# A fused adaLN, linear-attention and SwiGLU kernel: w_phi on ScalarE's queue, x's second chunk as one early load, silu and BD on GpSimd, and a new static order

## The chip, the cores and the metric

The kernel runs on one core of a Trainium2 chip. The metric is device time in microseconds of one launch. "Before" took 199.31 us (median of three runs, 198.96 to 199.45). The profile is one execution on the same chip, with a trace of every instruction of the engines: TensorE (PE, its weight loads PEld), VectorE (DVE), ScalarE (ACT), GpSimd (POOL) and SyncE (SP), which issues most of the DMAs.

## What is computed

One transformer layer on x of 2048 tokens by 512, in bf16. Six vectors of 512 come from a conditioning row c; they shift, scale and gate the two halves:

```python
mod = silu(c) @ w_mod                       # 6 x 512: sa, ca, ga, sb, cb, gb
h = layernorm(x) * (1 + ca) + sa
q, k, v = heads(h @ wqkv)                   # 32 heads of 16
pq, pk = q @ w_phi, k @ w_phi               # one 16x16 matrix per head
phi_q = concat(softmax(pq), softmax(-pq)); phi_k likewise
kv = phi_k.T @ v;  z = phi_k.sum(tokens)
o = (phi_q @ kv) / (phi_q @ z + 1e-6)
x = x + ga * (o @ wo)
h = layernorm(x) * (1 + cb) + sb
x = x + gb * ((silu(h @ w_gate) * (h @ w_up)) @ w_down)   # inner width 1376
```

## The kernel before

**Tiling.** The tokens are 16 tiles of 128, in four chunks of four tiles (x_c0 to x_c3, called x0 to x3 here). Weights stay in SBUF. All matmuls are bf16 into six one-bank PSUM tiles (one_ps) and a two-bank one (kv_ps).

**Start.** silu(c) is made as follows: four 1-row matmuls turn c into columns (L450), ScalarE takes exp(-c) into sig (L459), VectorE adds one, takes the reciprocal and multiplies (L454 to L456, f_silu). w_mod's first two parts then give modA, the shift and scale of the first half: eight 128x1 matmuls for each of four slices of 128 rows (L473), and a copy on VectorE (L478). Meanwhile w_phi is folded into wk: 16 small matmuls spread w_phi over the partitions (phx, L499), VectorE multiplies with a mask to the block-diagonal BD (L502), TensorE transposes wk (L519), ScalarE or VectorE copies it out (WT, L523), TensorE multiplies with BD (L530), and ScalarE or VectorE copies the folded wk back (L533, L534). wq is folded likewise a little later, with its transposes by DMA (L292).

**First norm.** For each tile VectorE takes bn_stats and their aggregate (L348, L349). The reciprocal root is taken by ScalarE (Ln, Exp, L377 and L378) or by GpSimd (power, L381 and L382), a reduction on VectorE gives the negative product with the mean (L384), and the normalize into xn runs on GpSimd, ScalarE or VectorE (L398, L396, L392). The tiles 0 to 5 are transposed by TensorE (L563, L414) and shifted and scaled on their way out of PSUM into hT (L566, L567, L422); the tiles from 6 on are transposed by DMA (L577) and shifted and scaled from SBUF (L585 to L590).

**K, V and Q.** Per tile: four matmuls for K (L619) and V (L623), two exponentials on ScalarE (L634), sums on VectorE (S, L640), a reciprocal (L644 to L646), va on VectorE (L650), a large multiply of e on GpSimd (L657), and then eight matmuls that add to kv_ps (L663). Q tiles are alike (L686, L690, L694, L696, L697, L701), and their result is transposed by DMA into pT (L705). After tile 15's kv accumulation VectorE masks the sum into KVZ (L790, L792).

**Second half.** Attention per tile (L824), its reciprocal A (L827) and product (L828) on VectorE, a transpose, the projection by wo (L857, wo having been multiplied by the gate on GpSimd, L780), the residual, the second norm, and then the SwiGLU part in units of one, two or four tiles (L909 gate and up, L916 silu, L919 or L923 and L925 for the product, L955 for the last 96 columns, L987 down, L997 and L1001 for gate and residual, and the stores at L1007).

**What sets the order.** Every step is announced by pl.op(alternatives, reads, writes, us, fn). A step may have several alternatives, each an engine with a planned duration. ORDER is a list written out by hand: number // 4 is the step, in the sequence of the calls, and number % 4 the alternative taken. Plan.run walks ORDER, gives each step the earliest start that its planned durations allow, chooses PSUM and SBUF slots, and emits all instructions by planned start. Each engine, and SyncE's queue ("XBAR" in the plan), works in the sequence in which ORDER names its steps. Where the plan finds TensorE idle in the first 90 us, fill() adds matmuls of ones into unused PSUM space (L1054). "later" (L289) is a load that SyncE issues at the place that ORDER gives it. One load is outside the plan: c_row, issued by ScalarE at L286, ahead of its table load (L319).

The loads in SyncE's sequence before: x0 (512 KB), wk (512 KB), w_phi (16 KB, 128 bytes per partition), w_mod in three loads (512, 256, 256 KB), x1 in two loads of 256 KB, x2, wq, wv, x3 (512 KB each). Then wq's transposes, and later the rest of w_mod, wo, w_gate, w_up and w_down, among the transposes.

Of the kernel before, what the change touches and what calls it, by code (L numbers as in the profile page):

```python
# [7 lines left out]
BF16 = mybir.dt.bfloat16  # L8
# [6 lines left out]
P = 128  # L15
# [20 lines left out]
def fm_size(m):  # L36
# [5 lines left out]
DMA_LN1 = 6  # L42
FILL_FROM, FILL_TO, FILL = 1.3, 90.0, 0.85
# [3 lines left out]
    0, 4, 48, 188, 72, 80, 8, 12, 16, 76, 20, 60, 52, 204, 228, 84, 56, 220, 172, 64, 208, 89, 92, 98, 156, 232, 176, 224, 24, 212, 104, 180, 193,  # L47
    28, 161, 236, 100, 184, 240, 196, 108, 217, 40, 246, 112, 164, 148, 116, 120, 124, 153, 36, 250, 32, 200, 268, 140, 168, 132, 128, 276, 316,
    252, 272, 68, 260, 144, 280, 136, 520, 264, 256, 324, 285, 320, 524, 328, 44, 424, 488, 428, 288, 560, 528, 464, 380, 492, 333, 600, 568, 294,
    298, 480, 432, 300, 472, 484, 336, 564, 468, 476, 368, 496, 342, 308, 532, 436, 346, 536, 304, 500, 541, 392, 440, 348, 608, 312, 384, 548, 445,  # L50
    604, 572, 510, 388, 828, 768, 404, 577, 452, 772, 544, 872, 372, 820, 376, 812, 776, 1344, 584, 506, 552, 513, 940, 518, 448, 460, 408, 412,
    804, 362, 358, 456, 396, 580, 780, 366, 944, 816, 864, 354, 904, 596, 824, 400, 868, 556, 808, 640, 832, 636, 612, 785, 792, 592, 836, 840, 908,
    788, 617, 644, 588, 1020, 876, 704, 800, 1340, 858, 1028, 648, 1024, 950, 796, 624, 881, 916, 620, 652, 416, 629, 962, 953, 888, 632, 860, 958,
    853, 1060, 921, 736, 656, 912, 1032, 846, 1188, 884, 712, 708, 900, 928, 716, 964, 1037, 744, 1228, 1268, 740, 1276, 924, 660, 1044, 850, 896,
    1308, 748, 1304, 933, 1040, 664, 1192, 1232, 893, 1200, 1360, 420, 1052, 936, 1318, 668, 720, 988, 1272, 1056, 993, 1240, 1196, 1049, 752, 1352,
    1205, 1325, 1212, 1328, 1208, 1224, 1280, 1313, 1236, 1322, 1245, 1252, 1336, 1356, 1220, 1285, 1364, 1248, 1264, 724, 1520, 1600, 1217, 1524,
    1369, 1292, 1604, 1528, 1260, 1348, 1004, 1560, 728, 1257, 1288, 1372, 1297, 1532, 1300, 1008, 1376, 1608, 1612, 1384, 1537, 1544, 1540, 1564,
    1816, 1388, 1617, 1620, 1640, 968, 1552, 1381, 1644, 1572, 1556, 1064, 1549, 1624, 1652, 1577, 1632, 1568, 1124, 1584, 1332, 1132, 1128, 1648,
    1580, 1592, 1596, 972, 1657, 1136, 976, 672, 1660, 1068, 996, 1636, 1589, 756, 1664, 1629, 1672, 732, 1072, 1669, 1676, 676, 1824, 980, 760,
    1828, 1092, 680, 1001, 1832, 1100, 984, 1680, 1836, 684, 1856, 1860, 1096, 1076, 1812, 1864, 1156, 1104, 1108, 1160, 1808, 1744, 2164, 1820,  # L60
    2168, 764, 1080, 1084, 2172, 1868, 1872, 1392, 1164, 1876, 1400, 2176, 688, 1748, 1424, 1112, 1116, 1880, 2180, 1688, 2184, 1488, 692, 1088,
    1884, 1396, 1712, 1888, 1120, 2416, 1684, 2188, 1140, 696, 1168, 1432, 1892, 2420, 700, 1752, 1776, 2424, 1716, 1898, 1172, 1456, 1492, 1144,
    1496, 1148, 1012, 1720, 1908, 1428, 1912, 1464, 2428, 1900, 1904, 2432, 2216, 1176, 2192, 2436, 2220, 2224, 2196, 2012, 2440, 1784, 2228, 1936,
    1152, 2016, 1460, 1180, 1780, 2200, 1016, 2204, 1952, 1500, 1916, 2020, 2232, 1940, 1944, 1956, 2237, 1948, 2444, 2208, 2024, 1404, 1960, 1184,
    2214, 2468, 2028, 1436, 2512, 2516, 1964, 1920, 1968, 2240, 1504, 2032, 2520, 2257, 1988, 2472, 2250, 1972, 2524, 1992, 1408, 1976, 2448, 1440,
    2246, 2253, 2296, 1980, 2528, 2316, 1924, 2452, 2036, 1984, 2260, 2040, 2532, 1444, 2304, 1412, 1448, 1416, 1452, 2352, 2536, 2044, 2300, 2456,
    1928, 2476, 2324, 2320, 1508, 1420, 1788, 2048, 2460, 2280, 2328, 1692, 2936, 1512, 1932, 2052, 2264, 2308, 2480, 2284, 2940, 2540, 2268, 2272,
    2288, 2944, 2056, 1516, 2332, 2544, 2484, 2924, 2360, 2564, 2292, 1848, 2928, 2340, 2932, 1792, 2948, 2064, 2568, 2548, 2312, 2060, 2336, 1724,
    2552, 2490, 2368, 2068, 2344, 2088, 2465, 1996, 2356, 2104, 2572, 2576, 2348, 2392, 1696, 2364, 2976, 2580, 2000, 2128, 2096, 1468, 1472, 2585,
    2072, 2556, 1728, 2980, 1476, 2492, 2984, 2372, 2276, 2506, 2112, 1732, 2124, 1481, 2952, 1756, 2988, 2561, 2588, 2510, 2132, 3032, 3036, 2605,  # L70
    1700, 1484, 3040, 2594, 2956, 1796, 2376, 2396, 2092, 2498, 1704, 2400, 2601, 2108, 2501, 2597, 2992, 1736, 2136, 2076, 3020, 2380, 2704, 2808,
    3024, 2080, 2720, 3028, 2960, 2404, 2116, 2997, 2964, 2668, 2648, 2816, 2100, 3044, 2724, 1708, 2652, 1760, 2728, 1740, 2732, 2968, 2676, 2974,
    2664, 2672, 3072, 2680, 3048, 3076, 3444, 1764, 2656, 2712, 2812, 2736, 3080, 3000, 2608, 2120, 3448, 2756, 1801, 3452, 2820, 3432, 3052, 3084,
    1804, 3056, 2760, 2744, 3060, 2140, 2660, 2764, 2824, 2628, 2612, 3436, 2616, 3064, 3088, 2408, 2144, 3013, 3006, 3440, 2700, 2620, 2084, 3094,
    3009, 2772, 2768, 2708, 2740, 1768, 3069, 3456, 2632, 3540, 3096, 2004, 2780, 1853, 2776, 3544, 2784, 2716, 3460, 2148, 3105, 2152, 3484, 3101,
    3017, 3548, 3488, 3492, 2792, 2684, 1772, 2636, 2688, 2748, 3464, 3114, 3528, 3532, 3110, 2752, 2788, 3536, 2692, 3468, 2640, 3552, 2796, 3116,
    3472, 2800, 3268, 3264, 3212, 3220, 2008, 3272, 2696, 3120, 2804, 3136, 3140, 3496, 3208, 3500, 3276, 3144, 3556, 3560, 3172, 3244, 3564, 3216,
    3476, 3568, 2624, 3482, 3180, 3148, 3300, 2900, 3580, 3572, 3584, 3176, 3252, 2156, 3224, 2904, 3308, 2876, 3124, 2852, 3588, 3506, 3184, 2644,
    2412, 3592, 2880, 2884, 2385, 2908, 3508, 3284, 3152, 2912, 3188, 3304, 2856, 3292, 3280, 3248, 3596, 3312, 3602, 3525, 3192, 3256, 3578, 3288,
# [3 lines left out]
    3796, 2920, 3628, 3632, 3668, 3420, 3756, 3636, 3404, 3700, 2844, 3808, 3708, 2848, 3676, 3348, 3680, 3688, 3704, 3712, 3792, 3764, 3752, 3776,  # L83
    3760, 3812, 3372, 3696, 3772, 3800, 3740, 3816, 3736, 3376, 3768, 2896, 3780, 3824, 3804, 3660, 3424, 3828, 3380, 3744, 3748, 3784, 3844, 3848,
    3892, 3640, 3836, 3820, 3916, 3920, 3832, 3840, 3852, 3924, 3353, 3896, 3900, 3356, 3868, 3872, 3876, 3928, 3856, 3940, 3944, 3948, 3861, 3960,
    3964, 3968, 3933, 3904, 3428, 3909, 3864, 3880, 3952, 3936, 3912, 3885, 3972, 3976, 3956, 3888,
]


# [1004 lines left out]
```

## Time and profile before

| | before |
|---|---|
| median of three runs | 199.31 us (198.96 to 199.45) |
| the profiled execution | 199.18 us, its span 197.4 us |
| granted TensorE clock | 1.000 |
| busy in the span: TensorE, VectorE, ScalarE, GpSimd | 192.4, 136.3, 108.9, 126.0 us |
| moved by DMA | 24.16 MB, of it 11.58 MB read from HBM |

The span is the time from the first to the last instruction of the profiled execution; the 1.8 us between span and time lie around it. In the lists below a line of the timeline has the start, the duration from the first start to the last end of a run of like instructions, the engine, the line of the program, the operation, what it writes and reads, the shape, and how many there are. A line of the chain has the start, the length and the work that the end of the program goes back to at that moment.

### The profile page before, as it was taken

Reading aid. Unit: us, or ns where it says so; the run is one execution under the profiler, and the core shown is the slowest. Engines: PE = TensorE matmul, PEld = TensorE weight load, DVE = VectorE, ACT = ScalarE, POOL = GpSimd, SP = SyncE. Lnnn points to the kernel's source line nnn. Section 1 sums busy time; section 2 is a strip of 40 time slices with the busy share of each in tenths; the row PEclk is TensorE's granted clock in tenths of the full one; section 3 lists DMA queues with packets and bytes.
Section 4 is the critical chain, followed back from the end, with each engine's and each line's share of the span. In section 5 each row is a group of like instructions: output and inputs, shape, how many; then the busy total and the mean of one; then the engine's idle time right before and its main releaser. Section 6 shows DMA issues by size and latency. Waiting matters only on the chain.

```text
span 197.4 us, 4080 instructions
## 1 busy us (share of the span) xinstructions
PE 192.4 (97%) x1494; PEld 108.1 (55%) x1494; DVE 136.3 (69%) x268; ACT 108.9 (55%) x247; POOL 126.0 (64%) x207
## 2 busy tenths in 40 slices
PE   7999999999999999999999999999999999999993
PEld 2754555555754777967664555554444544544452
DVE  5999999999999899998973873844234203241453
ACT  2499999999769974366452452633145330134300
POOL 1469999999997667686763777657746420139200
DMA  6999789899928570836509157150370001021112
GB/s 203 334 381 151 129 201 355 186 310 392 203 53 162 107 151 13 167 66 110 99 14 188 37 100 82 30 130 0 66 103 20 27 0 53 3 66 40 47 38 76
DMA packets 51141, 24.16 MB, mean 122 GB/s; under 512 B 42449, under 2 KB 47922, under 8 KB 51122
## 3 DMA queue, kind: packets, MB, share of 16 engines
q1 hardware_dynamic: 50976, 23.88, 51.7%
q8 instruction: 11, 0.18, 0.4%
q14 instruction: 8, 0.07, 0.1%
q10 hardware_dynamic: 146, 0.03, 0.1%
HBM read 11.58 MB, written 2.10 MB: 69 GB/s over the span
## 4 chain that ended last, share of the span: by engine, by line
PE 93%; DMA 3%; DVE 1%; issue 1%; SPq 0%; DVEq 0%
PE one_ps L909 35%; PE one_ps L987 17%; PE one_ps L857 7%; PE one_ps L623 7%; PE one_ps L686 7%; PE one_ps L619 7%; PE one_ps L955 3%; DMA wk<-in_A_wqkv_dram 2%; PE kv_ps L663 2%; PE kv_ps L824 2%; PE kv_ps L1054 1%; DMA out_dram<-ot 1%; PE one_ps L530 1%; PE one_ps L473 1%; DVE fg L997 1%; PE one_ps L414 1%
## 5 line engine op out<-in xcount | busy, mean ns | idle before, releaser
L909 PE MATMUL one_ps<-hT,wgu_sb 128*128 128x512 bf16 (+2 forms) x480 | 74.5, 308 | 0.0
L909 PEld LDWEIGHTS <-wgu_sb 128*128 128x128 bf16 x480 | 40.3, 98 | 28.7
L916 ACT ACTIVATE sg<-one_ps 128x512 bf16<-128x512 f32 (+1 forms) x41 | 23.6, 586 | 37.2 <-PE one_ps L909 24.9
L987 PE MATMUL one_ps<-wd_sb,gu 128*128 128x512 bf16 (+1 forms) x160 | 37.8, 372 | 0.0
L925 POOL TENSOR_TENSOR gu<-usb,sg 128x512 bf16<-128x512 bf16 x19 | 22.1, 1168 | 24.2 <-ACT sg L916 12.2
L997 DVE TENSOR_TENSOR fg<-one_ps,gab 128x512 bf16<-128x512 f32 (+1 forms) x16 | 10.4, 667 | 23.8 <-PE one_ps L987 23.8
L919 DVE TENSOR_TENSOR gu<-one_ps,sg 128x512 bf16<-128x512 f32 (+1 forms) x22 | 14.2, 658 | 18.1 <-PE one_ps L909 11.1
L987 PEld LDWEIGHTS <-gu 128*128 128x128 bf16 x180 | 16.6, 98 | 16.0
L348 DVE BATCH_NORM_STATS2 st<-x_c 128x6 f32<-128x512 bf16 x32 | 21.3, 678 | 1.7 <-DMA x_c<-in_A_x_dram 1.5
L923 ACT CAST usb<-one_ps 128x512 bf16<-128x512 f32 x19 | 11.1, 586 | 18.2 <-PE one_ps L909 18.0
L640 DVE TENSOR_REDUCE S<-e 128x64 f32<-128x1024 bf16 x16 | 19.2, 1202 | 0.4 <-POOL e L657 0.2
L694 DVE TENSOR_REDUCE Sq<-eq 128x64 f32<-128x1024 bf16 x16 | 19.2, 1203 | 0.0
L690 ACT ACTIVATE eq<-one_ps 128x512 bf16<-128x512 f32 x32 | 17.1, 614 | 2.3 <-PE one_ps L686 2.2
L634 ACT ACTIVATE e<-one_ps 128x512 bf16<-128x512 f32 x32 | 17.0, 615 | 0.0
L657 POOL TENSOR_TENSOR e<-e,S 128x512 bf16<-128x512 bf16 x16 | 16.8, 1060 | 0.2
L857 PE MATMUL one_ps<-wo_sb,oT 128*128 128x512 bf16 x64 | 16.1, 379 | 0.0
L623 PE MATMUL one_ps<-wv,hT 128*128 128x512 bf16 x64 | 15.9, 379 | 0.0
L619 PE MATMUL one_ps<-wk,hT 128*128 128x512 bf16 x64 | 15.5, 379 | 0.0
L686 PE MATMUL one_ps<-wq,hT 128*128 128x512 bf16 x64 | 15.4, 379 | 0.0
L701 POOL TENSOR_TENSOR eq<-eq,Rq 128x512 bf16<-128x512 bf16 x14 | 14.8, 1059 | 0.4
L1001 POOL TENSOR_TENSOR ot<-x_c,fg 128x512 bf16<-128x512 bf16 x7 | 8.1, 1153 | 10.0 <-DVE fg L997 10.0
L860 DVE TENSOR_TENSOR x_c<-x_c,one_ps 128x512 bf16<-128x512 bf16 x16 | 10.7, 669 | 5.3 <-PE one_ps L857 5.1
(120 smaller groups left out, 279.7 us busy)
## 6 DMA issues: line engine op xcount, KB each, us to landing
wmod_sb<-in_w_mod_dram SPq DMA_DIRECT2D x2, 1024.0 KB, 7.8
out_dram<-ot SPq DMA_DIRECT2D x15, 128.0 KB, 1.9
x_c<-in_A_x_dram SPq DMA_DIRECT2D x3, 512.0 KB, 7.2
wgu_sb<-in_B_w_up_dram SPq DMA_DIRECT2D x1, 1376.0 KB, 10.9
wgu_sb<-in_B_w_gate_dram SPq DMA_DIRECT2D x1, 1376.0 KB, 13.4
wd_sb<-in_B_w_down_dram SPq DMA_DIRECT2D x1, 1280.0 KB, 7.5
wk<-in_A_wqkv_dram SPq DMA_DIRECT2D x1, 512.0 KB, 4.8
wmod_sb<-in_w_mod_dram SPq DMA_DIRECT2D x1, 512.0 KB, 5.9
```

The costliest lines, as they stand in the source:

```text
L348: pl.op("DVE", r=reads, w=[st6], us=0.6, fn=lambda: nc.vector.bn_stats(st6()[:], src))
L619: nc.tensor.matmul(pk()[:], lhsT=hT[c_i][k][:, cols], rhs=Wk2[:, k, :], start=(k == 0), stop=(k == KD - 1))
L623: nc.tensor.matmul(v()[:], lhsT=hT[c_i][k][:, cols], rhs=wv_sb[:, k, :], start=(k == 0), stop=(k == KD - 1))
L640: pl.op("DVE", r=[e], w=[Ss], us=1.13, fn=lambda: nc.vector.tensor_reduce(Ss()[:].rearrange("p g s h -> p (g s h)"), e()[:].rearrange("p g ...
L686: nc.tensor.matmul(pq()[:], lhsT=hT[c_i][k][:, cols], rhs=Wq2[:, k, :], start=(k == 0), stop=(k == KD - 1))
L690: pl.op("ACT", r=[pq, btab], w=[be[sg]], us=0.48, fn=lambda sg=sg: nc.scalar.activation(eq[:, :, sg].rearrange("p g h f -> p g (h f)"), pq ...
L694: pl.op("DVE", r=be, w=[Sq], us=1.13, fn=lambda: nc.vector.tensor_reduce(Sq()[:].rearrange("p g s h -> p (g s h)"), eq[:].rearrange("p g s ...
L857: nc.tensor.matmul(a()[:], lhsT=oT()[:, j0 + j, :], rhs=wo_sb[:, j, :], start=(j == 0), stop=(j == KD - 1))
L909: nc.tensor.matmul(ps_()[0:fsz, q * n:(q + 1) * n], lhsT=wgu_sb[:, k, i, m * P:m * P + fsz], rhs=h2[k], start=(k == 0), stop=(k == KD - 1))
L916: pl.op("ACT", r=[g, btab], w=[sg], us=0.08 + 0.41 * L / CW, fn=lambda: nc.scalar.activation(sg()[0:fsz, 0:L], g()[0:fsz, 0:L], ACT.Silu))
L925: pl.op("POOL", r=[usb, sg], w=[gu], us=0.17 + 0.98 * L / CW, fn=lambda: nc.gpsimd.tensor_tensor(gu()[0:fsz, 0:L], usb()[0:fsz, 0:L], sg() ...
L987: nc.tensor.matmul(fp()[:], lhsT=b()[0:fsz, c0:c0 + P], rhs=wd_[0:fsz, m, wcs], start=(m == 0), stop=(m == FM - 1))
```

## The change

- **Loads.** w_phi is loaded by ScalarE right after c_row, at the top of its queue, and no more by SyncE. x1 is one load of 512 KB. By the new ORDER the loads on SyncE's queue run: x0, x1, wk, w_mod in the same three loads, x2, wq, wv, x3.
- **silu.** ScalarE copies c's columns to SBUF (c_sb) ahead of the exponential. GpSimd then adds one (with an upper limit of 1e38), takes the power -1 and multiplies. In GpSimd's queue this is the first step of the plan; f_masks and BD follow, then the normalizes of tiles 1, 0, 3 and 2.
- **BD.** phx is copied to SBUF (by ScalarE in this order), and the multiply with the mask is GpSimd's in this order.
- **A new alternative.** Tile 0's A = 1/denominator may be made by ScalarE with Ln and Exp, and is in this order. A second new path (statistics on ScalarE, stats_act) is switched off: ACT_STATS is empty.
- **ORDER** is written anew, and with it many engines are chosen anew. At the start: both reciprocal roots of tiles 0 to 3 on ScalarE, that of tiles 8 to 11 on GpSimd; WT copies three on ScalarE and one on VectorE (before two and two), copies of the folded wk all four on ScalarE (before three and one); hT of tiles 0 and 1 all on VectorE (before three on ScalarE and one on VectorE); the statistics of x1 on VectorE ahead of modA's copy. On TensorE phx stands ahead of wk's transposes, tile 0's K ahead of tile 1's, and the transposes of tiles 2 and 3 ahead of one of tiles 0 and 1. One reciprocal (tile 0's R) moves from ScalarE to VectorE. The normalizes of the first norm are 15 on GpSimd and one on ScalarE (before 13, two and one on VectorE), the hT tiles of first_T seven on GpSimd and five on ScalarE (before nine and three). All four wo multiplies stand behind the last e multiply (before, one stood ahead). Later on, wo, w_up and w_down are loaded before the rest of w_mod, and w_gate after it. The last 12 matmul steps are the same as before; on VectorE tile 12's gate multiply comes ahead of tile 15's, and one half of tile 15's residual goes to GpSimd.
- The planned sizes of the loads (kb) and some planned durations are changed; they act on the plan only, and so on the number and places of the fillers.

```diff
+ACT_STATS = ()
+ACC = 0.8
+EARLY = 1
 ORDER = [
...
     nc.scalar.dma_start(c_row[:], c[:, :])
+    nc.scalar.dma_start(wphi_sb[:], A_w_phi.rearrange("h (q t) f -> (h q) (t f)", t=4))
...
+    mone = const.tile([P, KD], FP32, name="mone")
+    nc.gpsimd.memset(mone[:], -1.0)
...
-    later(x_ch[0][:], x_v[0], bx[0:4], 400)
-    later(Wk2[:], wqkv_v[:, :, D:2 * D], bwk[0:1], 690)
-    later(wphi_sb[:], A_w_phi.rearrange("h (q t) f -> (h q) (t f)", t=4), [bphi], 70)
-    for k, n, kb in ((0, 2, 770), (2, 1, 280), (3, 1, 280)):
+    later(x_ch[0][:], x_v[0], bx[0:4], 490)
+    later(Wk2[:], wqkv_v[:, :, D:2 * D], bwk[0:1], 540)
+    for k, n, kb in ((0, 2, 560), (2, 1, 255), (3, 1, 255)):
         later(wmod_sb[:, k:k + n, 0:2 * D], wmod_v[:, k:k + n, 0:2 * D], bm1[k:k + n], kb)
-    for t in (0, 2):
-        later(x_ch[1][:, t:t + 2, :], x_v[1][:, t:t + 2, :], bx[TPC + t:TPC + t + 2], 270)
+    later(x_ch[1][:], x_v[1], bx[TPC:2 * TPC], 510)
...
+    def f_sig():
+        nc.scalar.copy(c_sb[:], cT()[:])
+        nc.scalar.activation(sig[:], cT()[:], ACT.Exp, scale=-1.0)
+
     def f_silu():
-        nc.vector.tensor_scalar_add(sig[:], sig[:], 1.0)
-        nc.vector.reciprocal(rsig[:], sig[:])
-        nc.vector.tensor_tensor(silucT[:], rsig[:], cT()[:], op=ALU.mult)
+        nc.gpsimd.tensor_scalar(sig[:], sig[:], 1.0, 1e38, op0=ALU.add, op1=ALU.min)
+        nc.gpsimd.tensor_tensor(rsig[:], sig[:], mone[:, 0:KD], op=ALU.pow)
+        nc.gpsimd.tensor_tensor(silucT[:], rsig[:], c_sb[:], op=ALU.mult)
...
-    pl.op("DVE*", r=[bsig, cT], w=[bsil], us=0.5, fn=f_silu)
+    pl.op("POOL", r=[bsig], w=[bsil], us=1.5, fn=f_silu)
...
-    pl.op("DVE", r=[phx], w=[bBD], us=0.6, fn=lambda: nc.vector.tensor_tensor(
-        BD[:], phx()[:].rearrange("p (j f) -> p j f", f=DH).unsqueeze(2).to_broadcast([P, KD, 8, DH]),
-        bm128[:].unsqueeze(1).to_broadcast([P, KD, 8, DH]), op=ALU.mult))
+    pl.op([("ACT", 0.14, lambda: nc.scalar.copy(ph_sb[:], phx()[:])),
+           ("DVE", 0.13, lambda: nc.vector.tensor_copy(ph_sb[:], phx()[:]))], r=[phx], w=[bph])
...
+    pl.op([("POOL", 1.05, lambda: f_bd(nc.gpsimd)), ("DVE*", 0.6, lambda: f_bd(nc.vector))], r=[bph], w=[bBD])
...
-        pl.op("DVE", r=[nd], w=[A], us=0.26, fn=lambda: nc.vector.reciprocal(A()[:], ndv()[:, :, HG:NDW]))
+        alts = [("DVE", 0.26, lambda: nc.vector.reciprocal(A()[:], ndv()[:, :, HG:NDW]))]
...
+        def fa():
+            nc.scalar.activation(A()[:], ndv()[:, :, HG:NDW], ACT.Ln)
+            nc.scalar.activation(A()[:], A()[:], ACT.Exp, scale=-1.0)
+        if n < EARLY:
+            alts.append(("ACT", 0.43, fa))
```

## The prediction

> **What bounds the kernel now.** I read the page first (busy shares and slices), then the chain of waits in order of time, the busy time by stage, and the timeline of the first 26 us and around 53 us.
>
> ```profile
> PE 192.4 (97%) x1494; PEld 108.1 (55%) x1494; DVE 136.3 (69%) x268; ACT 108.9 (55%) x247; POOL 126.0 (64%) x207
> ```
>
> TensorE is busy almost throughout. So the time is the moment at which useful matmuls start, plus their sum, plus what stands between them, plus the tail. The chain says where those moments are:
>
> ```profile
> 1.18 4.83 DMA wk<-in_A_wqkv_dram
> ...
> 11.80 0.55 PE kv_ps L1054 x3
> 12.35 1.73 PE one_ps L619 x8
> 14.08 0.08 PE kv_ps L1054
> 15.89 0.16 PE kv_ps L1054
> ...
> 189.12 0.40 issue
> ```
>
> L1054 are filler matmuls that the kernel puts where its plan has TensorE idle. The first K projection (L619) starts at 12.35. From there to 189.12 nothing is on the chain but matmuls, and only five fillers (0.08, 0.16, 0.22, 0.20, 0.10 = 0.76 us, all before 24.05) are no use. So the change can win only three things: an earlier first K, those 0.76 us, and the tail after 189.12 (8.3 us).
>
> ```profile
> 4.40:4.80 0.40, 0.40 (x3) 0.12 (x2) 0.40 (x2) 0.00 (x0) 0.00 (x0) 1.00 0.98 348
> 5.20:5.60 0.40, 0.40 (x3) 0.10 (x1) 0.40 (x3) 0.00 (x0) 0.00 (x0) 1.00 0.98 86
> 5.60:6.00 0.40, 0.09 (x2) 0.00 (x0) 0.40 (x2) 0.00 (x0) 0.00 (x0) 1.00 0.38 121
> 6.40:6.80 0.40, 0.40 (x19) 0.40 (x17) 0.29 (x3) 0.00 (x0) 0.32 (x2) 1.00 1.02 399
> 26.00:60.00 34.00, 34.00 (x345) 18.77 (x342) 33.57 (x47) 30.35 (x88) 33.77 (x52) 1.00 0.91 244
> ```
>
> Columns: stretch, length, busy PE, PEld, DVE, ACT, POOL, granted clock, DMA share, GB/s. Two things: from 5.2 to 6.0 the loads run at about 100 GB/s and not 348 to 399, while w_phi's packets (128 bytes each) go through; and from 26 to 60 us VectorE and GpSimd are as full as TensorE. The granted clock is 1.00 in every row.
>
> ```profile
> 9.83 0.34 PE L473 MATMUL one_ps<-silucT,wmod_sb 128*128 128x1 bf16 x8
> 10.21 0.17 DVE L478 COPY modA<-one_ps 128x8 f32<-128x8 f32 x1 [0.48 <-PE one_ps L473]
> 10.51 1.50 ACT L566 ACTIVATE hT<-one_ps,modA 128x256 bf16<-128x256 bf16 x3
> 12.19 1.89 PE L619 MATMUL one_ps<-wk,hT 128*128 128x512 bf16 x8
> 21.04 1.06 POOL L657 TENSOR_TENSOR e<-e,S 128x512 bf16<-128x512 bf16 x1
> 51.85 1.06 POOL L657 TENSOR_TENSOR e<-e,S 128x512 bf16<-128x512 bf16 x1
> 53.06 0.42 PE L663 MATMUL kv_ps<-va,e 128*128 128x68 bf16 x8
> 53.82 0.68 DVE L792 TENSOR_TENSOR KVZ<-kv_ps,bm 128x512 bf16<-128x512 f32 x1
> 55.04 0.42 PE L824 MATMUL kv_ps<-KVZ,pT 128*128 128x68 bf16 x8
> ```
>
> The start is a chain: last slice of w_mod, L473, modA, four hT tiles, K. At 53 us the last kv accumulation (L663) starts 0.15 us after GpSimd's last multiply (ends 52.91), and attention (L824) 0.54 us after KVZ (ends 54.50). GpSimd has no slack there, VectorE half a microsecond.
>
> **Loads.** Before, landings (issue plus time to landing) are x0 4.1, wk 6.0, w_phi 6.15, w_mod 8.1, 8.8 and 9.5, second half of x1 about 10.6. After, x1's 512 KB go ahead of wk. At 394 GB/s (mean of 2.4 to 3.2 us, 4 KB runs) that is 1.33 us; wk's 512 KB at 340 GB/s (3.6 to 4.8 us) are 1.54: wk lands at 4.1+1.33+1.54 = 7.0, one later. w_mod's 1 MB at 395 GB/s is 2.65: last slice at 9.65, if w_phi's hole (0.8 us at 100 GB/s, so about 0.6 us lost) vanishes from this queue, and 10.3 if it is only moved ahead. Here a rule speaks against the change: the Trainium skill's "DMA: Bandwidth & Descriptors", section "Issuing engines are not separate DMA queues", says that loads from several queues run on the same engines, and that a second queue saves only the issue. By it the saving is w_phi's issue (0.50 us on SyncE), which hides nothing here as loads queue anyway: 10.3. By the row, the loss is in packets standing in line with wk's tail, with DMA share down to 0.38, so engines idle: 9.65. I take 9.9, nearer the row. ScalarE pays one issue of 0.5 us; its table load (1.27 to 2.55) ends by 3.1, ahead of sig at 3.55: hidden.
>
> **First K.** L473 0.34, modA 0.17 and hops: hT from about 10.55 instead of 10.41. All four hT tiles are now VectorE's (0.41 each, about 0.37 apart) and TensorE starts on K once two are there: about 11.5; its second half waits for the fourth (12.1). The other arms must be ready: wk at 7.0, then seven ScalarE copies (before: two in 1.07, three in 1.56, so 0.53 each) from 7.5 to 11.2, the two that K's first half needs by 10.7. VectorE from x0 at 4.1: eight bn_stats (about 0.61 apart), aggregates, two reductions, one WT copy = 6.1 us, to 10.2, just ahead of modA. This arm has 0.3 us of cover; x0 late by more moves K one to one. The first two K tiles are done at 13.5 instead of 14.08: **-0.6** (between -0.85 and +0.2, by the last slice at 9.65 or at 10.3 with x0 late too).
>
> **Fillers.** Three of the five (0.52 us, 21 to 24 us) stand ahead of tiles of x1, whose hT GpSimd made at 22.1 to 24.6 (L589). x1 lands 5 us sooner, but wq's fold and wv come no earlier than by the 0.6. I take **-0.3** (0 to -0.76).
>
> **Silu, BD, and the moved steps.** GpSimd's row for the power is 0.72 (128x2), for small multiplies 0.24 to 0.26: silu about 1.3 us against 0.48 on VectorE. BD costs 1.06 on GpSimd by L657, the same form, against 0.67 (L502). ("GPSIMD Engine Reference" of the skill, "4.1 Engine selection", says about twice VectorE, so 1.34; the row decides, 0.3 less.) Both lie in GpSimd's idle stretch (it waits until 6.25 before), and cost nothing if w_phi lands by 4.9 (phx 0.55, copy 0.2, BD 1.06, hops 0.3 before the first normalize at 7.0). Queued behind them are the four normalizes of tiles 0 to 3. w_phi as late as 6.15 delays these by 1.3 us, of which 0.2 reaches K. The same wait has two more places: TensorE stands at phx (second in its queue, with wk's transposes behind it, which can't start before 7.0), and ScalarE at the copy of phx (behind it the first Ln for tiles 0 and 1, ready at 6.2). So w_phi by 5.3 costs nothing there, and 6.15 moves the Ln by 0.7 us, the same 0.2 at K. ScalarE's added copy of c (0.17, like L459) is hidden before 6 us.
>
> VectorE before KVZ: minus silu 0.48, BD 0.67, a WT copy 0.40, a Wk copy 0.68, a normalize 0.40, plus three hT 1.23, one reciprocal 0.5 and modB's copy 0.15: -0.75. With 0.54 of slack it lets attention start up to 1.3 us earlier. So it doesn't eat the 0.9.
>
> GpSimd from its first to its last e multiply: 33.7 us of work before (summed by rows in the order's sequence), 32.7 after: an eq multiply with its ratio more (1.34), two hT tiles (1.12) and a wo multiply (1.16) less. Ahead of the first e multiply it waits for statistics of x2: x1's normalizes run at about 12.3 to 15.7 (before 14.88 to 18), x2's by 20.7, so that multiply starts at about 20.8 (before 21.04), and the last one ends some 1.2 us earlier. No new wait on L663.
>
> Tile 0's reciprocal (L827, 0.34 on VectorE) becomes two ScalarE steps (0.27 and 0.26 by L644, L645), behind ScalarE's exponentials. It heads the chain to the first L857, whose weight load waited 0.43 for oT: **+0.1** (0 to +0.4).
>
> The weights now queue otherwise on SyncE: wo, w_up and w_down (3.2 MB, some 8.3 us at 380 GB/s) go ahead of the transposes of tiles 12 to 15. These wait for GpSimd's normalizes at about 32 anyway, and the loads can start at 22: 0 (to +0.5). The tail keeps its last 12 matmul steps; half a residual (1.15 on GpSimd against 0.42) is early enough to be off the end: 0.
>
> **Sum.** -0.6 - 0.3 + 0.1 = -0.8. The profiled execution took 199.18 (span 197.4, and 1.8 around it), 0.13 under the median of 199.31, so no correction: 199.31 - 0.8 = 198.5.
>
> **Rivals.**
> (1) A wash, chance 0.2: the hole moves with w_phi, x0 is late, K starts within 0.2 of before, or the gain is won and lost at a later wait (VectorE's half microsecond at KVZ). For it: the DMA share is 0.9 to 1.1 from 2.4 us on, so nothing is free there. Against it: 0.38 within the hole. 199.2.
> (2) Slower, chance 0.2: GpSimd becomes the bound. It gets 2.4 us of new work ahead of its normalizes, and twelve of these now stand before its first e multiply, waiting for VectorE's reductions. It is full from there to 53.9 us, so delay is passed on. The point: with 1.0 us less to do, L663 is later than before once the first e multiply starts after 22.0; each microsecond beyond costs one. Started at 22.9 (w_phi at 6.2 and x2's reductions behind two S reductions of 1.2 each), it gives 200.2. For it: 33.77 busy of 34. Against it: its idle time before 14.9 us is nearly 8 us.
> (3) The change does not do what it says: the ScalarE queue is served no sooner, w_phi lands at 6 again. It stays within (1).
>
> **How the numbers follow.** The main case has 0.6, at 198.5, its own range 197.9 to 198.9. A measurement tells 0.3% (0.6 us) from no change. Faster by over that (under 198.7): 0.47 of the main case and 0.03 of the wash, 0.50. Same: 0.13 + 0.15 = 0.28. Slower: 0.20 + 0.02 = 0.22. The range 197.7 to 200.1 takes in the fillers and the hole at their good ends, and half of rival (2).
>
> **What would show it.** wk landing at 7.0 and w_mod's last slice at 9.9; no stretch near 100 GB/s in the first 10 us; first L619 piece at about 11.5; fillers after the first K under 0.5; first e multiply on GpSimd before 21; L663's last set at about 52.3. Wrong if TensorE's chain has gaps between 26 and 189, or if modA is copied after 10.9.

## The result, and the profile after

The changed kernel takes 200.38 us (median of six runs, 199.86 to 201.19), the kernel before 199.32 beside it: ratio 1.0061, 95% interval 1.0036 to 1.0086. It is slower, by 1.06 us, where the prediction had 0.8 us faster. The profiled execution took 200.38, its span is 198.6, 1.2 longer than before.

The chain of waits after, in order of time; L1095 are the fillers, L509 is phx, L535 wk's transposes, L483 the modulation, L653 is K:

```profile
0.72 0.52 ACTq L289
1.27 4.42 DMA wphi_sb<-in_A_w_phi_dram
5.74 0.60 PE one_ps L509 x16
6.33 2.57 PE kv_ps L1095 x6
8.91 1.47 PE one_ps L535 x16
...
13.77 0.59 PE one_ps L653 x2
14.36 0.22 PE kv_ps L1095
...
194.18 0.50 issue
```

The chain no longer begins with wk but with w_phi, and first K stands at 13.77, where it was at 12.19 before (12.19 is its start in the timeline; the chain shows 12.35). From there on the chain is matmuls again, as before. So the loss is made in the first 14 us. The rows by stretch (columns as in the prediction):

```profile
4.40:4.80 0.40, 0.03 (x1) 0.00 (x0) 0.40 (x2) 0.00 (x0) 0.40 (x1) 1.00 1.02 357
4.80:5.20 0.40, 0.00 (x0) 0.00 (x0) 0.40 (x2) 0.00 (x0) 0.40 (x1) 1.00 0.73 227
5.20:5.60 0.40, 0.00 (x0) 0.00 (x0) 0.40 (x2) 0.00 (x0) 0.32 (x4) 1.00 0.96 328
6.40:6.80 0.40, 0.40 (x2) 0.15 (x1) 0.40 (x3) 0.38 (x2) 0.14 (x1) 1.00 1.01 366
26.00:60.00 34.00, 33.71 (x339) 18.82 (x341) 33.39 (x47) 30.71 (x89) 33.63 (x52) 1.00 0.85 239
```

The stretch at 100 GB/s is gone; from 2.4 us on the lowest row is 227. (The 33.71 of 34 in the last row come of records that this trace lacks: without fillers it has 1446 matmuls, the trace of before 1468. The chain has no gap there.) In its place TensorE does nothing from 4.43 to 5.74, and at 6.4 to 6.8 it gets through two matmuls where it made 19 before (of smaller ones). The timeline of the same places:

```profile
5.74 0.60 PE L509 MATMUL one_ps<-wphi_sb,spread 128*128 128x16 bf16 x16 [1.31 <-DMA wphi_sb<-in_A_w_phi_dram]
6.18 2.72 PE L1095 MATMUL kv_ps<-ones 128*128 128x512 bf16 x6
8.70 1.67 PE L535 MATMUL one_ps<-ident_b,wk 128*128 128x128 bf16 x16
12.25 0.34 PE L483 MATMUL one_ps<-silucT,wmod_sb 128*128 128x1 bf16 x8
12.63 0.17 DVE L488 COPY modA<-one_ps 128x8 f32<-128x8 f32 x1 [0.34 <-PE one_ps L483]
12.93 1.37 DVE L601 TENSOR_SCALAR hT<-one_ps,modA 128x256 bf16<-128x256 bf16 x4
13.77 0.59 PE L653 MATMUL one_ps<-wk,hT 128*128 128x512 bf16 x2
22.76 1.07 POOL L691 TENSOR_TENSOR e<-e,S 128x512 bf16<-128x512 bf16 x1
51.70 2.08 POOL L691 TENSOR_TENSOR e<-e,S 128x512 bf16<-128x512 bf16 x2
53.96 0.67 PE L697 MATMUL kv_ps<-va,e 128*128 128x68 bf16 x16
55.19 0.68 DVE L826 TENSOR_TENSOR KVZ<-kv_ps,bm 128x512 bf16<-128x512 f32 x1
56.19 0.42 PE L858 MATMUL kv_ps<-KVZ,pT 128*128 128x68 bf16 x8
```

Attention starts 1.15 later than before (56.19 against 55.04), and the rest of the span, 142.4, is as long as before: the second half neither lost nor won. Six 512-column fillers take 2.57 us, 428 ns each; before, three took 0.81 at 7.36. wk had landed at 7.94 (issued at 1.65, 6.3 to landing), but its transposes wait behind those fillers until 8.7 and then run at about 100 ns each.

### The profile page after: what moved, and what is told of

Read it like the earlier page. It is cut to its first block, busy times and chain, and to the rows that moved or that the text cites. A ratio compares the mean times of both kernels' runs of the same rounds, so it can differ in the third digit from the quotient of the medians.

```text
span 198.6 us, 4037 instructions
## 1 busy us (share of the span) xinstructions
PE 191.3 (96%) x1463; PEld 108.3 (55%) x1486; DVE 137.9 (69%) x272; ACT 107.9 (54%) x245; POOL 124.5 (63%) x208
## 4 chain that ended last, share of the span: by engine, by line
PE 94%; DMA 2%; issue 1%; DVE 0%; ACTq 0%; DVEq 0%
PE one_ps L950 35%; PE one_ps L1028 18%; PE one_ps L653 7%; PE one_ps L720 7%; PE one_ps L657 7%; PE one_ps L898 7%; PE one_ps L996 3%; DMA wphi_sb<-in_A_w_phi_dram 2%; PE kv_ps L858 2%; PE kv_ps L697 2%; PE kv_ps L1095 2%; PE one_ps L546 1%; PE one_ps L483 1%; PE one_ps L535 1%; PE one_ps L420 1%
## 5 line engine op out<-in xcount | busy, mean ns | idle before, releaser
L1028 PE MATMUL one_ps<-wd_sb,gu 128*128 128x512 bf16 (+1 forms) x153 | 38.4, 372 | 0.3
L957 ACT ACTIVATE sg<-one_ps 128x512 bf16<-128x512 f32 (+1 forms) x41 | 22.8, 586 | 24.7 <-PE one_ps L950 21.0
L1038 DVE TENSOR_TENSOR fg<-one_ps,gab 128x512 bf16<-128x512 f32 (+1 forms) x16 | 10.6, 663 | 12.9 <-PE one_ps L1028 12.7
L735 POOL TENSOR_TENSOR eq<-eq,Rq 128x512 bf16<-128x512 bf16 x15 | 15.9, 1065 | 0.3
L653 PE MATMUL one_ps<-wk,hT 128*128 128x512 bf16 x62 | 15.7, 379 | 0.2
L657 PE MATMUL one_ps<-wv,hT 128*128 128x512 bf16 x61 | 15.1, 379 | 0.2
L365 POOL TENSOR_SCALAR ln_neg<-ln 128x1 f32<-128x1 f32 x16 | 3.7, 229 | 14.3 <-DVE ln L355 13.7
## 6 DMA issues: line engine op xcount, KB each, us to landing
wd_sb<-in_B_w_down_dram SPq DMA_DIRECT2D x1, 1280.0 KB, 11.6
```

Source lines behind the costliest of these rows:

```text
L653: nc.tensor.matmul(pk()[:], lhsT=hT[c_i][k][:, cols], rhs=Wk2[:, k, :], start=(k == 0), stop=(k == KD - 1))
L657: nc.tensor.matmul(v()[:], lhsT=hT[c_i][k][:, cols], rhs=wv_sb[:, k, :], start=(k == 0), stop=(k == KD - 1))
L957: pl.op("ACT", r=[g, btab], w=[sg], us=0.08 + 0.41 * L / CW, fn=lambda: nc.scalar.activation(sg()[0:fsz, 0:L], g()[0:fsz, 0:L], ACT.Silu))
L1028: nc.tensor.matmul(fp()[:], lhsT=b()[0:fsz, c0:c0 + P], rhs=wd_[0:fsz, m, wcs], start=(m == 0), stop=(m == FM - 1))
```

## The experiments

Theory A from these traces: TensorE works through its queue in order. phx is second in it, and w_phi lands at 5.7. The plan believed 4.0, so it put the fillers for the wait behind phx instead of ahead of it. TensorE stands idle for 1.3 us, before it has reached its full rate; it stays at half rate until about 10 us (512-column matmuls start 427 ns apart until then and 216 after); wk's transposes are late and slow. Rivals: GpSimd (the prediction's second rival), or the loads by themselves.

The table holds all runs, each with its ratio to the kernel before on the same chip, and the time and first K of its own profiled execution, and their difference ("rest"): what it took from first K to the end, with the 1.8 us around the span. The profiled execution can lie off the median, g1's by 1.4 us.

| kernel | median us | ratio, 95% interval | profiled | first K | rest |
|---|---|---|---|---|---|
| before | 199.3 | | 199.18 | 12.19 | 186.99 |
| after | 200.38 | 1.0061 (1.0036 to 1.0086) | 200.38 | 13.77 | 186.61 |
| e1 w_phi planned late | 199.80 | 1.0015 (0.9997 to 1.0032) | 199.74 | 11.66 | 188.08 |
| e3 e1, x1 behind w_mod | 201.98 | 1.0132 (1.0106 to 1.0158) | 202.19 | 15.57 | 186.62 |
| b1 before, w_phi by ScalarE | 199.72 | 1.0019 (1.0010 to 1.0029) | 200.08 | 12.79 | 187.29 |
| b2 before, x1 early | 201.89 | 1.0127 (1.0113 to 1.0142) | 201.80 | 14.82 | 186.98 |
| f2 after, no fillers behind phx | 201.63 | 1.0107 (1.0070 to 1.0145) | 201.19 | 13.79 | 187.40 |
| g1 e1, GpSimd relieved | 199.51 | 1.0006 (0.9989 to 1.0023) | 200.90 | 12.57 | 188.33 |
| g2 after, GpSimd relieved | 200.77 | 1.0057 (1.0042 to 1.0073) | 201.30 | 14.70 | 186.60 |
| g3 before, GpSimd relieved | 199.34 | 0.9995 (0.9987 to 1.0004) | 199.32 | 12.44 | 186.88 |
| h1 after, w_phi ahead of c_row | 200.32 | 1.0051 (1.0034 to 1.0068) | 200.13 | 13.48 | 186.65 |
| h2 e1, wk ahead of x1 | 200.05 | 1.0032 (1.0021 to 1.0043) | 199.77 | 11.56 | 188.21 |
| h6 e1, old order from 12 us | 199.60 | 1.0010 (0.9995 to 1.0024) | 199.79 | 12.46 | 187.33 |
| h7 h2 and h6 | 199.74 | 1.0015 (1.0003 to 1.0028) | 199.99 | 12.72 | 187.27 |
| k1 before, idle at the start | 201.01 | 1.0078 (1.0065 to 1.0090) | 201.01 | 14.11 | 186.90 |
| k6 h2, VectorE relieved | 199.91 | 1.0023 (1.0012 to 1.0034) | 200.36 | 12.72 | 187.64 |
| k7 h2, both relieved | 199.98 | 1.0036 (1.0016 to 1.0057) | 200.02 | 12.57 | 187.45 |
| k8 e1, silu and BD on VectorE | 199.68 | 1.0017 (1.0003 to 1.0031) | 199.64 | 13.02 | 186.62 |
| l1 before, w_phi first | 199.99 | 1.0036 (1.0021 to 1.0050) | 199.90 | 12.69 | 187.21 |
| l2 before, w_phi second | 200.20 | 1.0065 (1.0024 to 1.0106) | 199.68 | 12.75 | 186.93 |

### What the stop at phx costs

**e1**, the changed kernel with `bphi = Buf(at=5.8)` for `at=4.0`: the plan knows when w_phi lands and puts its fillers ahead of phx.

> The changed kernel with one number altered: the plan is told that w_phi arrives at 5.8 us and not at 4.0, so that the fillers that it puts between phx and wk's transposes stand ahead of phx. Loads, engines and order are those of the changed kernel. Theory A (TensorE stands at phx until w_phi lands at 5.7; the fillers behind phx, planned for the wait for wk, then run late and at the slow rate, and push wk's transposes from 8.0 to 8.9): TensorE is not idle from 4.4 to 5.7, the transposes start as wk lands (about 8.0) and take 0.9 instead of 1.5, the first K starts at about 12.5 instead of 13.8, time about 199.2. Theory B (x1's load ahead of wk and w_mod is the cost; wk and w_mod's last slice land at 8.0 and 10.6, the rest follows): first K at 13.3 or later, time 200.0 to 200.4.

Its TensorE timeline:

```profile
3.44 2.56 PE L1095 MATMUL kv_ps<-ones 128*128 128x512 bf16 x6
5.84 0.55 PE L509 MATMUL one_ps<-wphi_sb,spread 128*128 128x16 bf16 x16
7.09 1.07 PE L535 MATMUL one_ps<-ident_b,wk 128*128 128x128 bf16 x16 [0.26 <-DMA wk<-in_A_wqkv_dram]
11.66 0.59 PE L653 MATMUL one_ps<-wk,hT 128*128 128x512 bf16 x2
```

No stop, transposes at 1.07 instead of 1.67, first K at 11.66 where the prediction had 11.5. Part of the 2.1 us by which it is earlier than in after is luck of this execution, as wk landed at 7.04 in it and at 7.94 in after. With wk at 7.96 (g1, which has the same start) first K is at 12.57: so the stop alone costs 1.2 us at K. But the median falls by 0.6 only, not to the 199.2 expected, and stays above before's. The first half of the cause is found, and a second question opened.

**k1** tests the rate alone, in the kernel before, where no load and no order changes: the fillers between c's turn and wk's transposes are left out (`if early and 3.0 < t0 < 6.0: return` in fill). They compute nothing.

> The kernel before without the fillers that TensorE has between the turn of c (ends 3.52) and wk's transposes (5.7 to 6.1); loads, order and all else as before. The fillers compute nothing that is used. Theory E (an idle stretch early on keeps TensorE at half rate for some four microseconds more): wk's 16 transposes and phx run at about 107 ns each instead of 55, fold and K's start come late, first K at 12.8 to 13.6 instead of 12.2, and the time rises by 0.5 to 1.2, to 199.9 to 200.6. If the rate does not depend on the idle stretch: 199.3, first K at 12.2.

201.01, more than expected: 2.5 us without useless work cost 1.7 us. TensorE's timeline, first of before, then of k1:

```profile
6.06 0.40 PE L519 MATMUL one_ps<-ident_b,wk 128*128 128x128 bf16 x4 [0.37 <-DMA wk<-in_A_wqkv_dram]
6.70 0.83 PE L519 MATMUL one_ps<-ident_b,wk 128*128 128x128 bf16 x12
7.36 0.81 PE L1054 MATMUL kv_ps<-ones 128*128 128x512 bf16 x3
```

```profile
6.07 0.61 PE L519 MATMUL one_ps<-ident_b,wk 128*128 128x128 bf16 x4 [2.55 <-DMA wk<-in_A_wqkv_dram]
6.96 1.44 PE L519 MATMUL one_ps<-ident_b,wk 128*128 128x128 bf16 x12
8.19 1.49 PE L1056 MATMUL kv_ps<-ones 128*128 128x512 bf16 x3
```

The first of them starts at the same moment, and the same instructions take 1.5 to 1.8 times as long. The row by stretch does not show it as a clock: from 6.07 to 10.00 both have TensorE busy throughout and a granted clock of 1.00, but before makes 85 matmuls there and k1 39:

```profile
6.07:10.00 3.93, 3.93 (x85) 3.46 (x86) 3.51 (x15) 2.50 (x6) 2.50 (x5) 1.00 1.03 390
```

```profile
6.07:10.00 3.93, 3.93 (x39) 2.94 (x39) 3.05 (x14) 1.47 (x4) 2.35 (x4) 1.00 1.00 374
```

The trace's own clock record says why: in k1 it begins at 10.79, with full speed, and nothing is recorded ahead of it; the rows count a stretch without a record as 1.00. The trace of before has no clock record at all, so the 1.00 in its rows, which the prediction went by, says nothing about the start.

**f2**, the changed kernel without the six fillers behind phx (`if o.n == 38: return`):

> The changed kernel without the six fillers that TensorE has between phx and the first transpose of wk; the fillers behind the transposes, the order and the loads stay. Theory A (the start is lost in TensorE's own queue: phx late, then 2.6 us of fillers that end 0.95 after wk has landed, then transposes at the slow rate): the transposes start with wk, first K some 0.9 earlier than 13.77 if wk lands at 7.95 again, and the time falls by 0.4 to 0.9, to 199.5 to 200.0; the transposes still take about 1.5 us, or longer, as TensorE stands idle ahead of them. Rival B (the loads set the start, the fillers lie in time that is lost anyway): first K and time stay, 200.4.

Theory A had the fillers as a part of the cost, and that part failed: 201.63, slower still. wk's transposes start when wk lands, at 8.02, but take 1.89, and first K is at 13.79, where it was. What is won at the fillers is lost again at half rate:

```profile
5.64 0.58 PE L509 MATMUL one_ps<-wphi_sb,spread 128*128 128x16 bf16 x16 [1.21 <-DMA wphi_sb<-in_A_w_phi_dram]
8.02 1.89 PE L535 MATMUL one_ps<-ident_b,wk 128*128 128x128 bf16 x16 [1.80 <-DMA wk<-in_A_wqkv_dram]
```

By the clock records full speed begins at 10.78 here and at 9.98 in after. That the fillers bring it forward is not shown, though: in g2, which starts as after does and has these fillers, it begins at 11.73. Nor is it shown why f2's median is 1.2 us above after's with the same first K; its trace has one stall at 102 us.

**h1**, the changed kernel with w_phi's load ahead of c_row's:

> The changed kernel with the two loads at the top of ScalarE's queue exchanged: w_phi ahead of c_row, nothing else. The prediction said that w_phi landed by 5.3 costs nothing. Theory E (what costs is that TensorE, stopped at phx, loses the busy stretch after which it runs at the full rate): w_phi lands about 0.5 earlier, at 5.2 to 5.4, TensorE still stands from 4.4 on, now also for c_row, and still runs at 634 ns per 512-column filler until about 9 to 10 us; first K after 13, time within 0.4 of 200.4. Rival F (the cost grows in proportion to the wait at phx): wait and cost fall by half a microsecond, time 199.9 or less.

200.32, as theory E said. w_phi lands at 4.7, but now c_row lands late and the stop is ahead of c's turn:

```profile
4.66 0.26 PE L454 MATMUL one_ps<-ones,c_row 1*128 1x1 bf16 x4 [1.34 <-DMA c_row<-in_c_dram]
5.63 0.62 PE L509 MATMUL one_ps<-wphi_sb,spread 128*128 128x16 bf16 x16
6.10 2.72 PE L1095 MATMUL kv_ps<-ones 128*128 128x512 bf16 x6
8.61 1.48 PE L535 MATMUL one_ps<-ident_b,wk 128*128 128x128 bf16 x16
```

wk had landed at 7.24 here; it waits 1.4 us for fillers at half rate. Where the stop lies and for whom does not matter. Rival F, a cost that grows with the length of the stop, was not tested by this: the stop is as long as in after (1.34 and 1.31).

### Is it GpSimd?

The prediction's second rival had 200.2 from a first e multiply at 22.9; it is at 22.76, and the time is 200.38. That fits, so it was tested. In **g1** (on e1), **g2** (on after) and **g3** (on before) GpSimd multiplies only half of e's columns for tiles 2, 3 and 4 (`e()[:, 0:h, 1]`, h = G // 2) and leaves the other half out.

> The kernel with w_phi planned at 5.8 (first K at 11.66), and the multiply of e on GpSimd for tiles 2, 3 and 4 covers half of the columns only, about 0.53 us less each, 1.6 us of GpSimd's work ahead of the last kv accumulation; the second halves of these e stay unscaled. Theory C (what the earlier K wins is given back because GpSimd is full from its first to its last e multiply): the time falls by 0.5 to 1.0, from 199.8 to 198.8 to 199.3, and the gaps of TensorE at 25 to 40 us shrink. Rival D (it is given back at VectorE or in the second half): within 0.3 of 199.8.

> The changed kernel with the same half multiplies for tiles 2, 3 and 4 (their second halves stay unscaled). By the second rival of the prediction (GpSimd, begun at 22.76 with its first e multiply, sets the end): 200.4 falls to 199.3 or less. By theory A (TensorE's own late start, with nothing but matmuls on its chain from 13.8 us on, sets it): the last kv accumulation may come earlier, but the time stays within 0.3 of 200.4.

> The kernel before with the same half multiplies for tiles 2, 3 and 4 (their second halves stay unscaled). TensorE's chain is whole there from 12.35 on, so the time should stay at 199.3, within 0.3. If it falls by more, GpSimd sets the end of the first half in the kernel before too, and a chain of matmuls hides waits that stand behind GpSimd.

1.6 us less of GpSimd's work moves none of the three: 199.51 (from 199.80, the intervals overlap), 200.77 (from 200.38) and 199.34 (from 199.3). The rival is refuted: it had the right number for a wrong reason. GpSimd was late because everything was: from first K to the start of its first e multiply are 8.99 us in after and g2, 8.85 in before.

**k8** is e1 with silu and BD's multiply back on VectorE (`pl.op("DVE*", ...)` for silu, 61 for 60 in ORDER).

> The kernel with w_phi planned at 5.8 (199.8), with silu (three steps) and the multiply for BD put back on VectorE, in their new places in the order; the copies of c and of phx stay. The prediction held that their move to GpSimd costs nothing: then within 0.3 of 199.8, or somewhat more as VectorE gets 1.15 us. If the power and the multiply on GpSimd delay its normalizes and with them K: first K and the time fall by 0.3 or more.

199.68 against 199.80: as the prediction held, silu and BD cost nothing where they are. At the start the move is even a gain: with both on VectorE first K comes 5.51 us after wk's transposes begin, 4.57 in e1. The time shows none of this gain, which leads to the last question below.

### The loads

**e3** is e1 with x1's load behind w_mod's (in ORDER, 20 behind 16):

> As e1_phx_late, and x1's load goes behind w_mod's three, as before the change (still one load). Theory A: with phx out of the way x1's place matters little, since VectorE and GpSimd use x1 early; within 0.3 us of e1_phx_late, either way. Theory B: wk lands 1.4 us sooner (about 6.5), w_mod's last slice at about 9.3, first K at 11.8 to 12.2, time 198.7 to 199.0, 1.2 us under e1_phx_late.

201.98, 2.2 us above e1 and outside both expectations: x1 lands at 11.23, and VectorE stands at its statistics, ahead of the WT copy. With the new order x1 must be early.

**b2** is the reverse, the kernel before with x1's two loads ahead of wk:

> The kernel before with another part alone: the two loads of x1 go right behind x0, ahead of wk, w_phi and w_mod. Theory B: wk lands at about 7.6 and w_mod's last slice at about 10.6, first K about 1.1 us later, time 200.3. Theory A says of this only that TensorE has phx behind the first of wk's transposes here, so nothing but the landings delays it: 0.7 to 1.1 us.

201.89, 1.6 us more than expected: wk lands at 8.53, 2.5 later than before, and first K, at 14.82, is 2.6 later. In the old order wk must be early.

**b1** is the kernel before with w_phi by ScalarE and nothing else (`at=5.8`, so that the plan knows it).

> The kernel before with one part of the change: w_phi is loaded by ScalarE's queue behind c, no more by SyncE. If the slow stretch at 5.2 to 6.0 us (about 100 GB/s) belongs to w_phi's packets in SyncE's queue, it is gone: wk lands at about 5.6, w_mod's last slice at about 8.8, first K 0.3 to 0.6 us sooner, time 198.7 to 199.0. If the packets cost the same from any queue, the landings stay within 0.2 us and the time at 199.3.

No row is under 330 GB/s from 4.8 us on, wk lands at 5.8, w_mod's last slice at 8.5 instead of 9.4, and still first K is 0.6 later and the time 0.4 longer, against the expectation. TensorE ran at half rate until 7.6 in this profile (before until about 5), and its own queue, not w_mod, set the start. Two readings need care. The slow stretch is not in every execution of the old loads: k1 has it (127 and 119 GB/s, last slice at 9.6), g3 does not (lowest row 253, wk at 5.8, last slice at 8.9). And the moment of full speed moves too (6.55 in g3, with first K at 12.44), so one trace does not show why the median of b1's 19 runs is longer.

**l1** and **l2** are the kernel before with w_phi as first or as second load of SyncE's queue (in ORDER, 8 moved ahead).

> The kernel before with w_phi as the first load on SyncE's queue, ahead of x0 and wk, and no other edit. Its small packets then run while the other loads have hardly begun, instead of between wk and w_mod, where 5.2 to 6.0 us moved only 100 GB/s. If that hole costs time at the start: w_mod's last slice lands at 9.0 or before instead of 9.5, first K some 0.2 to 0.4 earlier, 198.9 to 199.2, though x0 lands half a microsecond later. If the hole is only moved (the engines stand at w_phi's packets wherever these are): x0 and wk land 0.5 to 0.8 later, first K after 12.4 and 199.3 to 199.9.

> The kernel before with w_phi between x0 and wk on SyncE's queue. x0 lands as before at 4.1, wk later by w_phi's packets (0.3 to 0.8). If the hole vanishes: w_mod's last slice by 9.0, first K 12.0 or earlier, 198.9 to 199.2. If it is only moved ahead of wk: wk at 6.5 or later, w_mod as before at 9.5, first K at 12.2 to 12.6 and 199.2 to 199.7.

199.99 and 200.20, neither faster. In l2 the rows from 4.8 to 6.4 fall to 164 to 241 GB/s and wk lands at 6.7, w_mod's last slice at 9.6 (before 9.4): the slow stretch is only moved. In l1 w_phi is there 1.8 us after its issue, but w_mod's last slice lands at about 10.

### Does an earlier first K pay?

**h2** (e1 with 4 ahead of 20 in ORDER: wk before x1), **h6** (e1 with the new ORDER up to a planned 12 us and the old one behind it) and **h7** (both):

> The kernel with w_phi planned at 5.8, and wk's load put ahead of x1's on SyncE's queue again, so x0, wk, x1, w_mod. wk should land at 5.9 to 6.5 instead of 7.05 to 7.95, x1 at about 7. Theory G (with TensorE warm, wk's late landing is what is left of the loss at the start): the start is then bound by the last slice of w_mod, first K at 11.3 to 11.8 in every execution, and the time falls from 199.5 to 199.8 to 199.0 to 199.3. Rival H (x1 as a part of w_mod's front sets modA by VectorE's statistics of x1, or what is won at K is lost in stalls later): first K may come early, but the time stays at 199.5 or more.

> The kernel with w_phi planned at 5.8 and the new order up to a planned 12 us, then the order and the engines of the kernel before for all that follows (A of tile 0 on VectorE again too). Theory I (the new order's later part gives back what the start wins, in stalls at 25 to 40 us and in the second half): TensorE has no gap over 0.15 after first K, and the time is 198.5 to 199.2. Rival J (the later part is neutral, the spread at the start decides): as the kernel with the new order throughout, 199.5 to 199.8.

> Both of the last two together: wk's load ahead of x1's, w_phi planned at 5.8, new order up to a planned 12 us and the order of before behind it. If G and I hold, 198.3 to 198.8, below both kernels; if only one of them, 199.0 to 199.4; if neither, 199.5 or more.

None beats the kernel before: 200.05, 199.60 and 199.74. h2 has first K at 11.56 and is no shorter than e1. The last column of the table says where the start's gain goes in the traced executions. In the old order the rest is 186.9 to 187.3, whether K starts at 12.2 or at 14.8. In the new one it is 186.6 when K starts at 13.0 or later (after, e3, g2, h1, k8; f2 has a stall at 102 us and 187.4), 0.4 less than before, but 187.4 to 188.3 when K starts between 11.5 and 12.8 (e1, g1, h2, k6, k7). The matmul starts show the stalls: spacing beyond that usual for their shape adds up to 0.14 us behind first K in after, none in before, h6 and h7, 1.41 in e1 and 1.54 in h2, half of it at 25 to 41 us and half at 72 or 100. In the list of TensorE's waits behind 13 us after and before have none; those of e1, h2 and g1:

```profile
PE one_ps L950 <- DVE hT L919: 0.5, 1, 0.5
```

```profile
PE kv_ps L858 <- DMA pT<-eq: 0.5, 1, 0.5
```

```profile
PE kv_ps L858 <- DMA pT<-eq: 0.7, 1, 0.7
PE one_ps L720 <- ACT e L668: 0.2, 1, 0.2
```

Behind these three waits stand VectorE, a DMA and ScalarE. In **k6** VectorE sums only half of the elements for S in tiles 0 to 3 (`[:, :, 0:w]`, w = DH // 2), in **k7** GpSimd is relieved as well:

> The kernel with wk's load ahead of x1's and w_phi planned at 5.8 (first K at 11.56, time 200.05), and the sums S of tiles 0 to 3 on VectorE run over half of the 16 elements only, about 0.6 us less each, 2.4 us of VectorE's work. Theory K (an earlier first K brings nothing as VectorE, full from 14 to 54 us, does not start earlier): the stalls of TensorE (1.54 us after first K) fall under 0.8 and the time to 199.4 or less. If GpSimd alone is what holds TensorE up: within 0.3 of 200.05.

> The same kernel with both relieved: the half sums of tiles 0 to 3 on VectorE and the half multiplies of e for tiles 2, 3 and 4 on GpSimd. If the two engines together hold up what the earlier K wins, the stalls nearly vanish and the time falls to 198.3 to 198.9, what the prediction's sum had said. If the stalls come from elsewhere (DMA transposes, ScalarE): 199.3 or more.

199.91 and 199.98, against 200.05. The stalls fall to 0.74 and 0.54, but in both profiles x1 landed at about 8.3 instead of 7.2 and first K was at 12.7 and 12.6, so the two can't be compared at one start. Which helper holds TensorE up is not settled; that TensorE waits more after an early start is seen in the stalls of five traces.

It is not so in every execution. Four of e1's 14 runs took 198.78 to 198.95, where of the 32 of before beside them only one is under 198.96 (198.90), and four took over 200. No trace was kept of a short one, so whether K was earlier in it or the stalls were missing is open.

## Why the prediction was wrong

- **w_phi, and TensorE at phx.** This step failed: "w_phi by 5.3 costs nothing there, and 6.15 moves the Ln by 0.7 us, the same 0.2 at K". w_phi landed at 5.7, and TensorE's stop cost 1.2 of the 2.3 us between the predicted first K and the real one (13.77 against 12.57 in g1, without a stop and with wk as late). The step counted who stands at phx and what lies behind, but not what TensorE does after standing, though fill() in the kernel reckons with 1200 columns per us ahead of a planned 7.0 us and 2400 after. By the profile of after the 1.2 are these: wk's transposes start 0.75 behind wk, for late fillers; and 0.5 more go from there to K (5.07 against 4.57 in e1 and g1), as they run at half rate. k1 shows the half rate alone at 1.7 us in the kernel before.
- **TensorE's rate at the start, which the prediction left out.** The Trainium skill's "TensorE: Matmul & The Clock Gate", Part 1, says that the array starts at half its clock and is released after some 3.4 to 4 us of sustained work. Here matmuls of 512 columns start 427 ns apart before the release and 216 after. By the clock records the release, the step to full rate, came between 4.5 and 7.6 us in the 14 profiles that have such a record and no stop (in before at 4.9, by spacing), which is 3.1 to 6.1 us after the first matmul at 1.44. In after, f2, g2, h1 and k1, with a stop of 1.2 to 2.55 us, it came between 9.5 and 11.7 (in after at 9.98), 4.2 to 5.8 us past the stop. The page has the clock taken back after an idle window of about 3.4 us; here shorter stops, ahead of the release, put it off. That they begin the count anew fits these figures, but nothing here shows how the count is kept. The moment is in part chance: after and g2 are the same up to 22 us, and were released at 9.98 and 11.73, with first K at 13.77 and 14.70, though wk landed 0.3 earlier in g2.
- **wk at 7.0.** This term was too small by 0.94, most of the rest of the 2.3. Only e1 had wk there (7.04). In the eight profiles with x0, x1, wk in this order it landed between 7.04 and 7.97, with the same issue times. What was transferred from 7.0 to 7.6 us, first in after, then in e1:

```profile
DMA packets 126, 0.24 MB, mean 394 GB/s; under 512 B 4, under 2 KB 17, under 8 KB 126
```

```profile
DMA packets 118, 0.24 MB, mean 399 GB/s; under 512 B 1, under 2 KB 1, under 8 KB 118
```

wk's packets are 1 KB and w_mod's 2 KB, so in after 13 of wk's 512 were still to come, and none in e1. In after the last 16 of them start one behind the other, about 43 ns apart, until 7.53; in e1 the last 16 start within 0.2 us, until 6.47. So the mean rate that the working took is right for nearly all of wk, and the landing waits for a few packets in single file. What holds these up was not found. Since the transposes of wk, not w_mod, head this kernel's chain to K, wk's landing moves K one to one (0.92 and 0.91 between e1 and g1).
- **w_mod's last slice at 9.9.** 9.76 in e1, 10.65 in after; modA was copied at 12.63, past the 10.9 that the prediction had named as a sign of being wrong. No stretch near 100 GB/s: right. b1 does not decide the question that was weighed there: with w_phi on another queue the last slice comes at 8.5, against 8.9 to 9.6 in g3, before and k1, so 0.4 to 1.1 us earlier by one trace, where the skill's rule grants the issue of 0.5. The saving is worth nothing here, as w_mod wasn't last.
- **Fillers, -0.3.** 0.34 us behind first K instead of 0.87, by spacing of starts: -0.5. The rest fell from 186.99 to 186.61. Right in this profile.
- **Silu and BD hidden.** Right (k8). The power took 1.05 us for 128x4, not 0.72, and BD 1.16, between the row's 1.06 and the 1.34 estimated by the page's rule.
- **GpSimd a microsecond shorter from first to last e multiply.** 31.02 against 31.88: -0.86. Right. Its first e multiply "at about 20.8" was 22.76 with the late K and 21.00 in e1.
- **The sum.** With K near 11.5 the time need not have been 198.5: e1 and h2, traced with first K at 11.66 and 11.56, took 199.74 and 199.77. The second failed step is the silent one, that a K that comes 0.6 earlier ends the program 0.6 earlier. The prediction had seen VectorE and GpSimd as full as TensorE from 26 to 60 us, checked their sums, and took them as enough. Which of them, or whether one of them, takes the gain is open.
- **Tile 0's A, the weights' queue, the tail, the second half.** No wait of TensorE behind them, and the second half as long as before: right within 0.1.

What stays open: why some packets of wk come late (and x1 in k6 and k7, against h2), what e1's short executions have that the traced one lacks, and which helper would have to be faster for a first K at 11.6 to pay.

## What to carry to other kernels

A moved load moves the instruction that waits for it: look at the in-order queue in which that instruction stands, and place fillers ahead of it, not behind. A short stop of TensorE early in a program can cost more than its own length, by the time at half rate that follows. And where several engines are full, do not count on an earlier start of one reaching the end: test it by the time from the first useful matmul to the end, at several starts and in more than one execution.

## What was not expected of the hardware

- Fillers that compute nothing are worth 1.7 us in the kernel before (k1). The granted clock of a row reads 1.00 at half rate as well; the spacing of matmuls tells, or where the trace's clock record begins. In the 19 traces that have one, its stretch at full speed is 187.73, 191.15 or 194.56 us long, which is 55, 56 and 57 times 3.413 us.
- A 512 KB load can be through but for a dozen packets and land 0.9 us later for these (wk in after against e1).
- w_phi's 16 KB in 128-byte packets land 1.8 us after issue as SyncE's first load (l1), 3.2 as its second (l2), 4.5 as its third (before), and 3.8 to 4.7 from ScalarE's queue, where it makes little difference to be first (4.0 in h1).
